# Written VectorE and ScalarE order, deferred elementwise tail, a third output buffer and shorter weight conversion in a fused RWKV6 + tanh-shrink kernel

## Chip, cores, metric

One core of a Trainium2 chip. The metric is the device time of one launch in microseconds (us), the median of the fast runs; an execution counts as slow when it takes over 1.5% longer than the fastest of the same kernel. Ratios are computed as the mean time of one kernel's fast runs over the mean of the other's fast runs of the same rounds, with a 95% interval, so they are not quite the ratio of the medians that are quoted beside them.

## The reference

A linear recurrence with a per-channel decay (RWKV6) feeds a two-layer dense block. All is fp32.

```python
# r, k, v, w: (B=4, H=8, S=768, D=48); u: (H, D); w_in: (384, 2048); w_out: (2048, 384)
for t in range(S):
    cur = einsum('bhd,bhe->bhde', u * k_t, v_t)
    y[:, :, t] = einsum('bhd,bhde->bhe', r_t, state + cur)
    state = w_t[..., None] * state + einsum('bhd,bhe->bhde', k_t, v_t)
x = y as (B*S, H*D)
h = x @ w_in
out = (h - tanh(h)) @ w_out
```

## The kernel before

The 3072 tokens are cut into eight blocks of 384. For each block the kernel runs 16 steps f. A step multiplies the block's x with one 128-column slice of w_in (`hp`), computes g = h - tanh(h) on ScalarE and VectorE, and accumulates g times a slice of w_out (`acc`) two steps later. Beside this, each step does one phase of the *next* block's recurrence: first-level scores, five score levels, transposes, state updates, results. All its matmuls write a PSUM tile named `att`, of which there is one buffer.

A score level: TensorE forms small products of `kq` and `rp`; VectorE copies them under a mask into the score matrix; VectorE then multiplies half of `kq` and half of `rp` by running decay products in place; and only then may TensorE form the next level.

```python
LAG = 2
def level(self, ps, m, p0, n):
    gr = self.gram(ps, self.tiles["kq"], self.tiles["rp"], p0, n, m, L // 2)   # TensorE -> att
    ...
    for h in range(2):
        nc.vector.copy_predicated(out=dst, mask=mask, data=src)               # score copies
def decay(self, m, p0, n):
    for t, half, by in ((self.tiles["kq"], 0, right), (self.tiles["rp"], 1, left)):
        nc.vector.tensor_tensor(out=part, in0=part, op=ALU.mult, in1=by...)    # decay products
    nc.vector.tensor_tensor(out=nxt, in0=left, in1=right, op=ALU.mult)         # next running product

def first(xT, f, ps):
    # three matmuls into hp, then
    nc.scalar.copy(out=h, in_=hp)
    nc.scalar.activation(out=s, in_=h, func=AF.Square)
    # qa, qb, th = tanh(h), big: four more on ScalarE
    nc.vector.scalar_tensor_tensor(out=hs, in0=h, scalar=SERIES, in1=s, ...)   # five operations that make g
    nc.vector.scalar_tensor_tensor(out=hs, in0=qa, ...)
    nc.vector.scalar_tensor_tensor(out=g, in0=qb, ...)
    nc.vector.tensor_tensor(out=th, in0=h, in1=th, op=ALU.subtract)
    nc.vector.copy_predicated(out=g, mask=big, data=th)
    return g
# ... after the last acc of a block:
    o = dense.tile([P, DM], F32, name="o", tag="o")                            # two buffers, three o per block
    nc.scalar.copy(out=o, in_=acc)
    nc.scalar.dma_start(out=out[r0:r0 + P, :], in_=o)

with tc.manual_schedule(engines={PE}):       # TensorE as written, the others by the framework's scheduler
    for i, blk in enumerate(blocks):
        for f in range(NF):
            if ready < NF: load_weights(ready)      # 64-bit weights to fp32: 2 ScalarE, 4 VectorE operations
            g = first(here, f, ps_d)
            next(run, None)                         # one phase of the next block's recurrence
            ...
```

## Time and profile before

| | before |
|---|---|
| median of the fast runs, us | 791.25 (786.39 to 792.87) |
| profiled execution: span, us | 789.3 |
| TensorE, VectorE, ScalarE busy | 88%, 71%, 60% |
| mean granted TensorE clock | 0.949 |
| start and block 0: hp(f=0) of block 1 begins at, us | 168.0 |
| a steady block (mean of blocks 1 to 5), us | 92.3 |

TensorE is busy 88% of the span, but "busy" hides two things: the waits between, and matmuls that run slowly after a wait. So the number to follow is the length of a steady block, from the start of its first hp matmul to the start of the next block's. The prediction below shows the lines. In them PE is TensorE, DVE VectorE, ACT ScalarE, POOL GpSimd and SP SyncE (a q behind the name: a transfer that this engine issues); a line gives start and duration in us, engine, source line, operation, what it writes and reads, shapes and how often, and in brackets the idle time before it and what ended it. The granted clock is the share of TensorE's full clock that the profile shows as allowed.

### The profile page before, as it was taken

How to read it: one execution, taken by the hardware profiler on the slowest of the kernel's cores; microseconds unless marked ns; L12 is line 12 of the kernel's file. 1: busy time of each engine (PE TensorE's matmuls, PEld its weight loads, DVE VectorE, ACT ScalarE, POOL GpSimd, SP SyncE). 2: the span in 40 equal slices, each digit the busy share in tenths (PEclk: the TensorE clock that was granted, in tenths of full speed). 3: DMA queues.
4: the chain of work that ended last, by engine and by line, in shares of the span. 5: the costliest groups of instructions: out<-in, count | busy, mean ns of one | idle time of the engine just before them, and what ended most of it. 6: DMA issues, size and time to landing. Idle time of an engine off the chain costs nothing.

```text
span 789.3 us, 20068 instructions
## 1 busy us (share of the span) xinstructions
PE 695.6 (88%) x8480; PEld 445.4 (56%) x8480; DVE 558.0 (71%) x1138; ACT 470.9 (60%) x955; POOL 18.8 (2%) x49
## 2 busy tenths in 40 slices
PE   3558688897999989997999979999898999999997
PEld 3544455655656556564655556565565656565554
DVE  7988988576775677667775777656777577656664
ACT  3528567375565656566375655655565664757775
POOL 5000000000000000000000000000000000000000
PEclk9988789898999989999899989999899999999999
DMA  8477223123013300133001230133001100000000
GB/s 286 176 238 239 85 81 121 52 71 108 2 41 119 102 12 2 42 119 110 2 10 62 90 112 2 41 115 105 12 2 42 48 32 3 1 9 26 5 0 30
DMA packets 30841, 54.36 MB, mean 69 GB/s; under 512 B 2336, under 2 KB 28704, under 8 KB 30752
## 3 DMA queue, kind: packets, MB, share of 16 engines
q1 hardware_dynamic: 24992, 35.79, 14.2%
q0 software_dynamic: 2304, 12.58, 4.7%
q10 hardware_dynamic: 3456, 4.72, 1.6%
q8 instruction: 66, 1.08, 0.6%
q14 instruction: 23, 0.19, 0.1%
HBM read 47.19 MB, written 4.72 MB: 66 GB/s over the span
## 4 chain that ended last, share of the span: by engine, by line
PE 51%; DVE 14%; ACT 10%; issue 7%; DMA 6%; PEld 5%; PEldq 1%; SPq 0%; ACTq 0%; DVEq 0%
PE acc L450 23%; PE hp L414 20%; PE att L220 6%; DMA out_y<-o 3%; DVE states L300 3%; ACT s L422 2%; DVE gT L436 2%; DVE gT L433 2%; DVE hs L431 2%; ACT h L421 2%; PEld att L315 2%; DMA raw<-in_weights 2%; DVE rp L241 2%; PE att L272 1%; ACT qa L423 1%
## 5 line engine op out<-in xcount | busy, mean ns | idle before, releaser
L450 PE MATMUL acc<-w_sb,gT 128*128 128x384 f32 x768 | 294.1, 521 | 5.4 <-ACT o L454 5.3
L414 PE MATMUL hp<-xT,w_sb 128*128 128x384 f32 x768 | 272.2, 491 | 9.0 <-DVE a L156 6.7
L414 PEld LDWEIGHTS hp<-xT,w_sb 128*128 128x128 f32 x768 | 147.7, 193 | 113.5 <-issue 14.4
L421 ACT COPY h<-hp 128x384 f32<-128x384 f32 x128 | 61.1, 477 | 235.9 <-PE hp L414 235.3
L450 PEld LDWEIGHTS acc<-w_sb,gT 128*128 128x128 f32 x768 | 145.4, 200 | 96.8 <-issue 11.6
L429 DVE SCALAR_TENSOR_TENSOR hs<-h,s 128x384 f32<-128x384 f32 x128 | 71.2, 556 | 163.1 <-ACT s L422 163.0
L220 PE MATMUL att<-rp,kq 48*64 48x32 f32 x3840 | 78.2, 241 | 44.6 <-DVE rp L241 44.0
L220 PEld LDWEIGHTS att<-rp,kq 48*64 48x64 f32 x3840 | 74.2, 161 | 64.7 <-issue 52.8
L436 DVE COPY_PREDICATED gT<-big,th 128x384 f32<-128x384 int32 x128 | 75.4, 589 | 7.7 <-DVE gT L433 0.9
L423 ACT ACTIVATE qa<-s,shift 128x384 f32<-128x384 f32 x128 | 77.0, 601 | 0.3
L433 DVE SCALAR_TENSOR_TENSOR gT<-qb,hs 128x384 f32<-128x384 f32 x128 | 71.3, 557 | 8.2
L424 ACT ACTIVATE qb<-s,shift 128x384 f32<-128x384 f32 x128 | 76.8, 600 | 0.0
L426 ACT ACTIVATE big<-s,shift 128x384 f32<-128x384 f32 x128 | 76.8, 600 | 0.0
L431 DVE SCALAR_TENSOR_TENSOR hs<-qa,hs 128x384 f32<-128x384 f32 x128 | 70.6, 552 | 0.3 <-ACT qa L423 0.3
L435 DVE TENSOR_TENSOR th<-h,th 128x384 f32<-128x384 f32 x128 | 70.5, 551 | 0.0
L422 ACT ACTIVATE s<-h 128x384 f32<-128x384 f32 x128 | 66.9, 523 | 3.6
L425 ACT ACTIVATE th<-h 128x384 f32<-128x384 f32 x128 | 64.9, 507 | 0.0
L263 DVE COPY_PREDICATED scores<-mask,att 128x384 f32<-128x384 uint8 (+1 forms) x72 | 43.5, 617 | 5.7 <-PE att L220 5.5
L241 DVE TENSOR_TENSOR kq<-kq,tot 128x768 f32<-128x768 f32 (+1 forms) x45 | 38.7, 860 | 0.3 <-PE att L220 0.3
L241 DVE TENSOR_TENSOR rp<-rp,tot 128x768 f32<-128x768 f32 (+1 forms) x45 | 38.7, 860 | 0.0
L300 DVE SCALAR_TENSOR_TENSOR states<-states,tot,att 128x48 f32<-128x48 f32 x176 | 34.9, 256 | 2.2 <-PE att L290 2.2
L315 PE MATMUL att<-rp,states 48*64 48x64 f32 x768 | 28.0, 230 | 9.2 <-DVE states L300 9.2
(45 smaller groups left out, 372.6 us busy)
## 6 DMA issues: line engine op xcount, KB each, us to landing
raw<-in_weights POOLq DMA_DIRECT2D x16, 768.0 KB, 4.7
rmix<-in_rT SPq DMA_DIRECT2D x7, 768.0 KB, 4.6
kmix<-in_kT SPq DMA_DIRECT2D x7, 768.0 KB, 6.3
wt<-in_wT SPq DMA_DIRECT2D x7, 768.0 KB, 4.6
kq<-in_kT SPq DMA_DIRECT2D x7, 768.0 KB, 4.5
rp<-in_rT SPq DMA_DIRECT2D x7, 768.0 KB, 4.7
v_sb<-in_v SPq DMA_DIRECT2D x8, 576.0 KB, 6.5
out_y<-o ACTq DMA_DIRECT2D x24, 192.0 KB, 1.9
```

What stands on the lines that cost most here:

```text
L220: nc.tensor.matmul(dst, lhsT=lhs[rows, t0:t0 + L], rhs=src, start=True, stop=True)
L241: nc.vector.tensor_tensor(out=part, in0=part, op=ALU.mult, in1=by.unsqueeze(2).to_broadcast([P, nblk, m]))
L414: nc.tensor.matmul(hp, lhsT=w_in_sb[:, f, kc, :], rhs=xT[:, kc, :], start=(kc == 0), stop=(kc == KC - 1))
L421: nc.scalar.copy(out=h, in_=hp)
L422: nc.scalar.activation(out=s, in_=h, func=AF.Square)
L423: nc.scalar.activation(out=qa, in_=s, func=AF.Square, bias=shift[:, 0:1])
L424: nc.scalar.activation(out=qb, in_=s, func=AF.Square, bias=shift[:, 1:2])
L426: nc.scalar.activation(out=big, in_=s, func=AF.Relu, bias=shift[:, 2:3])
L431: nc.vector.scalar_tensor_tensor(out=hs, in0=qa, scalar=QUAD[0][1], in1=hs, op0=ALU.add, op1=ALU.mult)
L433: nc.vector.scalar_tensor_tensor(out=g, in0=qb, scalar=QUAD[1][1], in1=hs, op0=ALU.add, op1=ALU.mult)
L436: nc.vector.copy_predicated(out=g, mask=big.bitcast(I32), data=th)
L450: nc.tensor.matmul(acc, lhsT=g[:, j * P:(j + 1) * P], rhs=w_out_sb[:, f, :], start=(f == 0), stop=(f == NF - 1))
```

## The change

The intent: keep VectorE from standing in front of TensorE. The five g operations are put off by one step (`rest`), so that they no longer wait for ScalarE in front of the score level; decay products come before score copies; the order is no longer the scheduler's but written, on VectorE and ScalarE; outputs and all other dense tiles have three buffers instead of two; loads for the next block but one are at step 10 (rp at 13); acc lags three steps; the weights are kept times 256, so that a clamp falls away from the conversion. The core of the diff:

```diff
-LAG = 2
+LAG = 3
-    dense = ctx.enter_context(tc.tile_pool(name="dense", bufs=2))
+    dense = ctx.enter_context(tc.tile_pool(name="dense", bufs=3))
...  conversion
-        nc.vector.tensor_scalar(out=a.bitcast(F32), in0=a.bitcast(F32), scalar1=LOWEST,
-                                scalar2=HIGHEST, op0=ALU.max, op1=ALU.min)
         nc.vector.tensor_single_scalar(a, a, 3, op=ALU.logical_shift_left)
...  level
         gr = self.gram(ps, self.tiles["kq"], self.tiles["rp"], p0, n, m, L // 2)
+        self.decay(m, p0, n)
...  first
-        nc.vector.scalar_tensor_tensor(out=hs, in0=h, ...)      # and the four that follow
-        return g
+        def rest():
+            nc.vector.scalar_tensor_tensor(out=hs, in0=h, ...)  # and the four that follow
+        return g, rest
...  main loop
-    with tc.manual_schedule(engines={PE}):
+    with tc.manual_schedule(engines={PE, DVE, ACT}):
-                g = first(here, f, ps_d)
+                g, next_rest = first(here, f, ps_d)
                 waiting.append((second, f, g))
-                next(run, None)
-                if f == PHASES and i + 2 < len(blocks):
-                    blocks[i + 2].load_all()
+                if rest:
+                    rest()
+                rest = next_rest
+                if later:
+                    later.phase(ps_a, f)
+                if after:
+                    after.prepare(f)          # loads at f == 10 and 13, mix and totals at 13
                 if len(waiting) > LAG:
                     s, fs, gs = waiting.pop(0)
                     s.add(fs, gs)
+                if i == 0 and f + AHEAD < NF:
+                    convert(*load_weights(f + AHEAD))
```

Cut from it: masks are built in one tile, zeros of the states are written by VectorE, the six small transfers that complete the first block's x (below, the hole transfers) go out on two queues, the last operations of the conversion change places, and the running decay products of a block are formed ahead of its first step.

More of the change, by code (lines that the diff above doesn't have):

```diff
@@ L42 @@
 PSUM = bass.MemoryType.PSUM
-PE = mybir.EngineType.PE
+PE, DVE, ACT = (getattr(mybir.EngineType, n) for n in ("PE", "DVE", "Activation"))
 B, H, S, D = 4, 8, 768, 48
@@ L61 @@
 BANK = 512
-PHASES = 14
-LAG = 2
+LAG = 3
 SMALL = 0.25
@@ L71 @@
 QUAD = ((0.6848211999739032, 6.0837500747262405), (-2.2310245716004378, 2.349190352486121))
-SCALE = 2.0 ** -48
-LOWEST = float(np.array(896 << 20, np.int32).view(np.float32)) * SCALE
-HIGHEST = float(np.array(1151 << 20, np.int32).view(np.float32)) * SCALE
+UPSCALE = 2.0 ** 8
+HIGH_SCALE = 2.0 ** -111
 @with_exitstack
@@ L96 @@
     xpool = ctx.enter_context(tc.tile_pool(name="xpool", bufs=2))
-    gpool = ctx.enter_context(tc.tile_pool(name="gpool", bufs=LAG + 2))
-    dense = ctx.enter_context(tc.tile_pool(name="dense", bufs=2))
+    gpool = ctx.enter_context(tc.tile_pool(name="gpool", bufs=LAG + 1))
+    dense = ctx.enter_context(tc.tile_pool(name="dense", bufs=3))
     conv = ctx.enter_context(tc.tile_pool(name="conv", bufs=2))
@@ L111 @@
     masks = {}
-    def make_mask(m, width, step):
-        nb = L // (2 * m)
-        t = const.tile([P, nb, width], I8, name=f"mask{m}", tag=f"mask{m}")
-        nc.gpsimd.memset(t, 1.0)
-        for par in range(2):
-            half = t[64 * par:64 * par + 64]
-            nc.gpsimd.affine_select(out=half, in_=half, compare_op=ALU.is_ge, fill=0.0, base=0,
-                                    pattern=[[-2 * m, nb], [0, width]], channel_multiplier=1)
-            nc.gpsimd.affine_select(out=half, in_=half, compare_op=ALU.is_ge, fill=0.0, base=m - 1,
-                                    pattern=[[2 * m, nb], [step, width]], channel_multiplier=-1)
-        masks[m] = t
-    make_mask(1, 2, 1)
+    mask_cols = {1: slice(0, 64), 2: slice(64, 96), 4: slice(96, 128), 8: slice(128, 160),
+                 16: slice(160, 192)}
+    mask_all = const.tile([P, 192], I8, name="mask_all", tag="mask_all")
+    nc.gpsimd.memset(mask_all[0:L], 1.0)
+    for m, at in mask_cols.items():
+        width, step = (2, 1) if m == 1 else (m, 0)
+        nb = L // (2 * m)
+        masks[m] = mask_all[:, at].rearrange("s (b j) -> s b j", j=width)
+        half = masks[m][0:L]
+        nc.gpsimd.affine_select(out=half, in_=half, compare_op=ALU.is_ge, fill=0.0, base=0,
+                                pattern=[[-2 * m, nb], [0, width]], channel_multiplier=1)
+        nc.gpsimd.affine_select(out=half, in_=half, compare_op=ALU.is_ge, fill=0.0, base=m - 1,
+                                pattern=[[2 * m, nb], [step, width]], channel_multiplier=-1)
+        if m == 1:
+            nc.gpsimd.tensor_copy(out=mask_all[L:P, at], in_=mask_all[0:L, at])
+    nc.gpsimd.tensor_copy(out=mask_all[L:P, 64:], in_=mask_all[0:L, 64:])
     A = const.tile([P, 2, NPAIR, NCP, L], F32, name="scores", tag="scores")
     nc.vector.memset(A, 0.0)
-    states = [const.tile([P, NPAIR, NCH, L], F32, name=f"states{q}", tag=f"states{q}")
-              for q in range(NQ)]
+    states = []
+    for q in range(NQ):
+        st = const.tile([P, NPAIR, NCH, L], F32, name=f"states{q}", tag=f"states{q}")
+        nc.vector.memset(st[:, :, :, D:], 0.0)
+        states.append(st)
+    nc.vector.memset(states[0][:, :, 0, :], 0.0)
     w_sb = const.tile([P, NF, 2 * DM], F32, name="w_sb", tag="w_sb")
@@ L150, in load_weights, with convert @@
         up = conv.tile([P, 2 * DM], I32, name="up", tag="up")
-        nc.scalar.activation(out=a.bitcast(F32), in_=hi.bitcast(F32), func=AF.Abs, scale=SCALE)
+        nc.scalar.activation(out=a.bitcast(F32), in_=hi.bitcast(F32), func=AF.Copy, scale=HIGH_SCALE)
         nc.scalar.activation(out=up, in_=lo.bitcast(U32), func=AF.Copy, scale=2.0 ** -29)
-        nc.vector.tensor_scalar(out=a.bitcast(F32), in0=a.bitcast(F32), scalar1=LOWEST,
-                                scalar2=HIGHEST, op0=ALU.max, op1=ALU.min)
+        return f, hi, a, up
+    def convert(f, hi, a, up):
         nc.vector.tensor_single_scalar(a, a, 3, op=ALU.logical_shift_left)
-        nc.vector.tensor_tensor(out=a, in0=a, in1=up, op=ALU.add)
-        nc.vector.scalar_tensor_tensor(out=w_sb[:, f, :].bitcast(I32), in0=hi, scalar=-2 ** 31, in1=a,
+        nc.vector.scalar_tensor_tensor(out=a, in0=hi, scalar=-2 ** 31, in1=a,
                                        op0=ALU.bitwise_and, op1=ALU.bitwise_or)
+        nc.vector.tensor_tensor(out=w_sb[:, f, :].bitcast(I32), in0=a, in1=up, op=ALU.add)
     fence, fences = tc.alloc_semaphore("fence"), []
@@ L230, in level_1, with totals, decay @@
                 data=gr.rearrange("s h (n t) -> s h n t", t=L))
-        def decay(self, m, p0, n):
+        def totals(self, m, p0, n):
+            cols = slice(p0 * NB, (p0 + n) * NB)
+            tot = self.tiles["wt"][:, cols] if m == 1 else self.tots[m, p0]
+            t2 = tot.rearrange("d (n two) -> d n two", two=2)
+            nxt = work.tile([P, n * NB // (2 * m)], F32, name=f"tot{2 * m}_{p0}_{n}", tag=f"tot{2 * m}_{p0}")
+            nc.vector.tensor_tensor(out=nxt, in0=t2[:, :, 0], in1=t2[:, :, 1], op=ALU.mult)
+            self.tots[2 * m, p0] = nxt
+        def decay(self, m, p0, n, which=("kq", "rp")):
             cols = slice(p0 * NB, (p0 + n) * NB)
@@ L237, in decay @@
             t2 = tot.rearrange("d (n two) -> d n two", two=2)
-            left, right = t2[:, :, 0], t2[:, :, 1]
-            for t, half, by in ((self.tiles["kq"], 0, right), (self.tiles["rp"], 1, left)):
-                part = t[:, cols].rearrange("d (n two m) -> d n two m", two=2, m=m)[:, :, half, :]
-                nc.vector.tensor_tensor(out=part, in0=part, op=ALU.mult,
-                                        in1=by.unsqueeze(2).to_broadcast([P, nblk, m]))
-            nxt = work.tile([P, nblk], F32, name=f"tot{2 * m}_{p0}_{n}", tag=f"tot{2 * m}_{p0}")
-            nc.vector.tensor_tensor(out=nxt, in0=left, in1=right, op=ALU.mult)
-            self.tots[2 * m, p0] = nxt
+            for name in which:
+                half = 0 if name == "kq" else 1
+                part = self.tiles[name][:, cols].rearrange(
+                    "d (n two m) -> d n two m", two=2, m=m)[:, :, half, :]
+                by = t2[:, :, 1 - half].unsqueeze(2).to_broadcast([P, nblk, m])
+                nc.vector.tensor_tensor(out=part, in0=part, in1=by, op=ALU.mult)
         def level(self, ps, m, p0, n):
             gr = self.gram(ps, self.tiles["kq"], self.tiles["rp"], p0, n, m, L // 2)
+            self.decay(m, p0, n)
             nb = L // (2 * m)
@@ L340, in result, with fill_holes @@
                 nc.scalar.copy(out=dst.rearrange("e (c a t) -> e c a t", a=2, t=L), in_=src)
-        def fill_holes(self):
+        def fill_holes(self, engines):
             for n in range(2 * KC):
@@ L346, in fill_holes @@
                 src = 64 * (n // KC) + 16 * (n % KC)
-                nc.sync.dma_start(out=self.xT[64 * h + D:64 * h + 64, i, :],
-                                  in_=self.late[src:src + 16, :])
-        def load_all(self):
-            for name, src in (("rmix", rT), ("kmix", kT), ("wt", wT), ("kq", kT), ("rp", rT)):
-                self.load(name, src, 0, NPAIR)
-            self.load_v()
-        def phases(self, ps):
-            self.mix(0, NPAIR, False)
-            for p0 in (0, UP):
-                self.level_1(ps, p0)
-                yield
-            m = 1
-            while m < L:
-                self.decay(m, 0, NPAIR)
-                m *= 2
-                if m < L:
-                    self.level(ps, m, 0, NPAIR)
-                    yield
-            for p0 in (0, UP):
-                self.turn(ps, p0)
-                yield
-                self.update(ps, p0, True)
-                yield
-            for p0 in (0, UP):
-                self.result(ps, p0)
-                yield
-            self.fill_holes()
-            yield
+                engines[n % len(engines)].dma_start(out=self.xT[64 * h + D:64 * h + 64, i, :],
+                                                    in_=self.late[src:src + 16, :])
@@ new lines, in phase @@
+        def phase(self, ps, k):
+            if k < 2:
+                self.level_1(ps, k * UP)
+                if k == 1:
+                    self.decay(1, 0, NPAIR, ("rp",))
+            elif k < 7:
+                self.level(ps, 2 ** (k - 1), 0, NPAIR)
+            elif k < 11:
+                p0 = (k - 7) // 2 * UP
+                if k % 2 == 1:
+                    self.turn(ps, p0)
+                else:
+                    self.update(ps, p0, True)
+            elif k < 13:
+                self.result(ps, (k - 11) * UP)
+                if k == 12:
+                    self.fill_holes([nc.sync])
@@ new lines, in prepare @@
+        def prepare(self, k):
+            if k == 10:
+                for name, src in (("rmix", rT), ("kmix", kT), ("wt", wT), ("kq", kT)):
+                    self.load(name, src, 0, NPAIR)
+                self.load_v()
+            elif k == 13:
+                self.load("rp", rT, 0, NPAIR)
+                self.mix(0, NPAIR, False)
+                for m in (1, 2, 4, 8, 16, 32):
+                    self.totals(m, 0, NPAIR)
+            elif k == 14:
+                self.decay(1, 0, NPAIR, ("kq",))
@@ L389, in start @@
                 self.level_1(ps, p0)
-            for m in (2, 4, 8, 16):
-                make_mask(m, m, 0)
+                self.decay(1, p0, UP)
+                self.totals(1, p0, UP)
             yield
-            m = 1
-            while m < L:
+            for m in (2, 4, 8, 16, 32):
                 for p0 in (0, UP):
-                    self.decay(m, p0, UP)
-                    if 2 * m < L:
-                        self.level(ps, 2 * m, p0, UP)
-                m *= 2
+                    self.level(ps, m, p0, UP)
+                    self.totals(m, p0, UP)
                 yield
@@ L406, in start @@
                 self.result(ps, p0)
-            self.fill_holes()
+            self.fill_holes([nc.sync, nc.scalar])
             yield
@@ L420, in first @@
         h, th, s, qa, qb, big = (new(n) for n in ("h", "th", "s", "qa", "qb", "big"))
-        nc.scalar.copy(out=h, in_=hp)
+        nc.scalar.activation(out=h, in_=hp, func=AF.Copy, scale=1.0 / UPSCALE)
         nc.scalar.activation(out=s, in_=h, func=AF.Square)
@@ L428, in first @@
         g = gpool.tile([P, NB], F32, name="gT", tag="gT")
-        nc.vector.scalar_tensor_tensor(out=hs, in0=h, scalar=SERIES, in1=s,
-                                       op0=ALU.mult, op1=ALU.mult)
-        nc.vector.scalar_tensor_tensor(out=hs, in0=qa, scalar=QUAD[0][1], in1=hs,
-                                       op0=ALU.add, op1=ALU.mult)
-        nc.vector.scalar_tensor_tensor(out=g, in0=qb, scalar=QUAD[1][1], in1=hs,
-                                       op0=ALU.add, op1=ALU.mult)
-        nc.vector.tensor_tensor(out=th, in0=h, in1=th, op=ALU.subtract)
-        nc.vector.copy_predicated(out=g, mask=big.bitcast(I32), data=th)
-        return g
+        def rest():
+            nc.vector.scalar_tensor_tensor(out=hs, in0=h, scalar=SERIES, in1=s,
+                                           op0=ALU.mult, op1=ALU.mult)
+            nc.vector.scalar_tensor_tensor(out=hs, in0=qa, scalar=QUAD[0][1], in1=hs,
+                                           op0=ALU.add, op1=ALU.mult)
+            nc.vector.scalar_tensor_tensor(out=g, in0=qb, scalar=QUAD[1][1], in1=hs,
+                                           op0=ALU.add, op1=ALU.mult)
+            nc.vector.tensor_tensor(out=th, in0=h, in1=th, op=ALU.subtract)
+            nc.vector.copy_predicated(out=g, mask=big.bitcast(I32), data=th)
+        return g, rest
     class Second:
@@ L453, in add @@
                     o = dense.tile([P, DM], F32, name="o", tag="o")
-                    nc.scalar.copy(out=o, in_=acc)
+                    nc.scalar.activation(out=o, in_=acc, func=AF.Copy, scale=1.0 / UPSCALE)
                     r0 = self.row0 + j * P
                     nc.scalar.dma_start(out=out[r0:r0 + P, :], in_=o)
-    with tc.manual_schedule(engines={PE}):
-        blocks = [Block(b, q) for b in range(B) for q in range(NQ)]
-        ready = 0
-        with tc.tile_pool(name="ps_boot", bufs=4, space=PSUM) as boot:
-            xT = blocks[0].begin()
-            for i, _ in enumerate(blocks[0].start(boot)):
-                if i == 0:
-                    for st in states:
-                        nc.gpsimd.memset(st, 0.0)
-                if i % 2 == 1:
-                    load_weights(ready)
-                    ready += 1
-            blocks[1].load_all()
-        ps_d = ctx.enter_context(tc.tile_pool(name="ps_d", bufs=1, space=PSUM))
-        ps_a = ctx.enter_context(tc.tile_pool(name="ps_a", bufs=1, space=PSUM))
-        waiting = []
-        for i, blk in enumerate(blocks):
-            here, run = xT, iter(())
-            if i + 1 < len(blocks):
-                xT = blocks[i + 1].begin()
-                run = blocks[i + 1].phases(ps_a)
@@ new lines @@
+    blocks = [Block(b, q) for b in range(B) for q in range(NQ)]
+    AHEAD = 4
+    with tc.manual_schedule(engines={PE}), \
+            tc.tile_pool(name="ps_boot", bufs=4, space=PSUM) as boot:
+        xT = blocks[0].begin()
+        for i, _ in enumerate(blocks[0].start(boot)):
+            if i % 2 == 1:
+                convert(*load_weights(i // 2))
+        blocks[1].prepare(10)
+    ps_d = ctx.enter_context(tc.tile_pool(name="ps_d", bufs=1, space=PSUM))
+    ps_a = ctx.enter_context(tc.tile_pool(name="ps_a", bufs=1, space=PSUM))
@@ L479 @@
+    with tc.manual_schedule(engines={PE, DVE, ACT}):
+        for k in (13, 14):
+            blocks[1].prepare(k)
+        waiting, rest, half_done = [], None, []
+        for i, blk in enumerate(blocks):
+            here = xT
+            later = blocks[i + 1] if i + 1 < len(blocks) else None
+            after = blocks[i + 2] if i + 2 < len(blocks) else None
+            if later:
+                xT = later.begin()
             second = Second(blk.b * S + blk.q * NB, ps_d)
             for f in range(NF):
-                if ready < NF:
-                    load_weights(ready)
-                    ready += 1
@@ L484 @@
-                g = first(here, f, ps_d)
+                g, next_rest = first(here, f, ps_d)
                 waiting.append((second, f, g))
-                next(run, None)
-                if f == PHASES and i + 2 < len(blocks):
-                    blocks[i + 2].load_all()
+                if rest:
+                    rest()
+                rest = next_rest
+                if later:
+                    later.phase(ps_a, f)
+                if after:
+                    after.prepare(f)
@@ L491 @@
                     s.add(fs, gs)
-            assert next(run, None) is None
+                if i == 0 and f + AHEAD < NF:
+                    convert(*load_weights(f + AHEAD))
+        rest()
         for s, fs, gs in waiting:
```

## The prediction

> **What bounds the kernel now.** I read the chain that ended last first (TensorE 51% of it, two matmul lines alone 43%), then the busy time of each engine by stretch, then who waited for whom, then the timeline of one steady block. A block is 384 tokens, 16 steps f. Each step has three first-layer matmuls (hp), some work of the next block's recurrence (att) and three second-layer matmuls (acc).
>
> Busy time by stretch: us, then busy us of PE, PEld, DVE, ACT and POOL, then the granted TensorE clock, DMA share and GB/s:
>
> ```profile
> 57.00:178.00 121.00, 102.58 (x1161) 64.95 (x1162) 98.08 (x190) 76.09 (x145) 4.78 (x9) 0.85 0.35 112
> 363.00:456.00 93.00, 84.97 (x1069) 53.85 (x1068) 63.63 (x133) 55.20 (x116) 0.00 (x0) 0.96 0.18 58
> 727.00:789.30 62.30, 56.24 (x173) 32.33 (x171) 37.10 (x70) 42.87 (x88) 0.00 (x0) 0.98 0.05 19
> ```
>
> The first row is mostly block 0, which also converts weights: VectorE is 81% busy and the clock is low. The second is a steady block: TensorE busy, VectorE at 68%. The third is mostly the last block, which has no recurrence beside it. From the TensorE timeline, hp(f=0) of blocks 0 to 7 starts at 57.0, 168.0, 260.7, 352.5, 445.3, 537.1, 629.7 and 716.8. So blocks 1 to 5 take 91.7 to 92.9 us each, block 6, beside which nothing is loaded for a later one, 87, and 72.5 us remain from the start of block 7 to the end.
>
> One steady block, TensorE only (start, us, what, number, idle before it and its releaser):
>
> ```profile
> 368.32 0.91 PE L450 MATMUL acc<-w_sb,gT 128*128 128x384 f32 x2 [1.05 <-ACT o L454]
> ...
> 374.72 2.79 PE L220 MATMUL att<-rp,kq 48*64 48x32 f32 x96 [3.55 <-DVE rp L241]
> 377.43 4.00 PE L450 MATMUL acc<-w_sb,gT 128*128 128x384 f32 x6
> 381.27 2.10 PE L414 MATMUL hp<-xT,w_sb 128*128 128x384 f32 x6
> 383.30 1.60 PE L220 MATMUL att<-rp,kq 48*64 48x32 f32 x96
> 384.83 2.20 PE L450 MATMUL acc<-w_sb,gT 128*128 128x384 f32 x6
> 386.87 2.10 PE L414 MATMUL hp<-xT,w_sb 128*128 128x384 f32 x6
> 389.72 1.60 PE L220 MATMUL att<-rp,kq 48*64 48x32 f32 x96 [0.75 <-DVE rp L241]
> ...
> 411.34 0.85 PE L272 MATMUL att<-ident,kq 128*128 128x128 f32 x6 [0.91 <-DVE states L300]
> ...
> 422.55 1.61 PE L315 MATMUL att<-rp,states 48*64 48x64 f32 x48 [1.58 <-DVE states L300]
> ```
>
> The bracketed idle times sum to 7.84 us. After the 3.55 us one, the same work is slower: att 2.79 instead of 1.60 (+1.19), acc 4.00 instead of 2.20 (+1.80). Together 10.8 us of a 92.5 us block. The origin is on ScalarE:
>
> ```profile
> 364.29 0.48 ACT L421 COPY h<-hp 128x384 f32<-128x384 f32 x1 [1.23 <-PE hp L414]
> 367.79 0.48 ACT L454 COPY o<-acc 128x384 f32<-128x384 f32 x1 [3.02 <-DMA out_y<-o]
> 368.17 0.53 ACT L422 ACTIVATE s<-h 128x384 f32<-128x384 f32 x1
> 368.72 0.56 DVE L429 SCALAR_TENSOR_TENSOR hs<-h,s 128x384 f32<-128x384 f32 x1 [4.54 <-ACT s L422]
> 373.62 0.95 DVE L241 TENSOR_TENSOR rp<-rp,tot 128x768 f32<-128x768 f32 x1
> ```
>
> The third output copy of a block finds both o buffers still being written out. ScalarE is in order, so s(f) behind it is late. VectorE is in order, its next item needs that s, and score copies and decay products stand behind it. So the decay ends at 374.6 and att starts at 374.72. Over the run:
>
> ```profile
> PE att L220 <- DVE rp L241: 44.0, 18, 7.4
> ...
> ACT o L454 <- DMA out_y<-o: 15.1, 6, 3.0
> ...
> PE att L315 <- DVE states L300: 9.2, 7, 2.3
> ...
> PE att L272 <- DVE states L300: 6.7, 7, 2.3
> ```
>
> **What the Trainium skill says.** "TensorE: Matmul & The Clock Gate", Part 1, says that an idle window of about 3.4 us puts the array at half clock until some 3.4 us of sustained work. The trace agrees: 2.79 against 1.60 us after 3.55 us idle, no slowing after 0.75. "DMA: Bandwidth & Descriptors" names a fixed cost of about 2 us, mostly the write receipt: the last output lands 1.9 us after issue, but those at block ends, beside two 768 KB loads, after 4.7 to 5.1. "Perfetto Trace Analysis", Engine Utilization, says that the same gap repeating can mean too few buffers; the o wait comes once per block, 6 times. "VectorE: DVE Perf Modes", The DRAIN you can't avoid, holds that a semaphore between chained operations costs nothing. The trace differs: independent 384-wide operations start 0.47 us apart, but the predicated copy starts 0.66 after the gT that it depends on, in the tail as well (780.91, 781.57).
>
> **The change, part by part.** The order listing confirms that TensorE keeps its instructions; only acc moves one step later (lag 3), and the same sequence is written for VectorE and ScalarE.
>
> (a) Three o buffers: the 3.0 us ScalarE wait and the 1.05 us TensorE wait go. The loads also move to steps 10 to 13, away from the output at step 2.
>
> (b) In a level step VectorE now does the five g operations of the step before, two decay products, two score copies. Start to start: products 0.86 each = 1.72; copies 0.47 each = 0.94 (1.62 for m=2, whose copies start 0.81 apart in this trace); the five g operations now have three dependent neighbours, 2 x 0.47 + 3 x 0.66 = 2.92. Sum 5.6. TensorE's level step is also 5.6 (383.30 to the would-be 388.9), so VectorE keeps up without slack in total. The link that matters is short: from the end of att, decay and copies need 1.72 + 0.94 + about 0.1 = 2.8 us (3.5 for m=2), while the next att comes 2.04 + 2.03 = 4.07 us later. The g operations come after, with ScalarE's chain done. I expect the decay wait to vanish.
>
> (c) State updates (12 x 0.175 = 2.1 us) no longer stand between g operations waiting for ScalarE: 2.1 + 0.1 fits into the 4.07 us before the transpose or result needs them. The 0.91 and 1.58 vanish.
>
> (d) So a steady block becomes its TensorE steps, start to start as the timeline has them where nothing waits: 5 level steps at 5.60 = 28.0; 2 first-level at 4.93 = 9.9; 2 transposes at 4.62 = 9.2; 2 updates at 4.92 = 9.8; 2 results at 6.58 = 13.2; 3 dense at 3.87 = 11.6. Sum 81.7. I take 82.2 for small waits. Blocks 1 to 6 took 548.8; six at 82.2 are 493: 56 us gained.
>
> (e) Weights. The min/max goes: 16 x about 0.5 = 8 us of VectorE, half of it before or in block 0's path. One conversion left is shift 0.66, sign 1.05, add 0.87 = 2.6. Block 0's level steps become 5.6 + 2.6 = 8.2 us against TensorE's 5.6: VectorE bounds there. Stepping it by hand from hp(0): steps 0 to 6 end (last decay) at about 53; conversions, g and two state updates carry result(11) to about 79; two results and three dense steps end near 102. Before it took 111. Gain 9. ScalarE (3.0 for a chain, 1.7 for a conversion) stays below.
>
> (f) Start: one min/max less in each of four conversions and one add later (2.8 us). The xT copies no longer stand behind a conversion that waits 2.77 us for raw. Six hole transfers go on two queues instead of one. hp(0), begun at 57.0 and whole only after 61, I put at 53.
>
> (g) End: lag 3 leaves four acc groups after the last hp instead of three, +1.9; the o waits of this stretch (1.02 at step 2, 1.03 at the end) go. Fifteen steps of 3.87, five groups of 1.94 and 3.9 from the last matmul to the end: 71.6 against 72.5.
>
> Sum: 53 + 102 + 493 + 71.6 = 719.6. The estimates of block 0 and the start add dependent costs generously, so I put **718 us**, 9% less.
>
> **Rivals.** R1: VectorE becomes the bound in steady blocks too. Its level step is 5.6 against 5.6; if copies or dependent pairs cost 0.5 us more, five steps in seven blocks add some 17 us: 735. For: the fixed order cannot fill an idle moment with something else. Against: steps outside the levels have 1 to 2 us to spare, and only the short link is on TensorE's path. R2: the fixed ScalarE order makes a new wait. Score and ks copies of steps 6 to 10 now stand behind the whole activation chain (3.0 us), ending at 3.8 to 4.6 us after hp against needs at 4.7 to 5.6; in block 0 the conversion waits there for raw. If 1 us per such step is lost, five per block: about 750. Against: before, ks was copied behind the chain as well (403.90, needed at 405.45) without a wait. R3: the TensorE waits were caused by the o wait alone, and orders matter little: then three buffers give the same block, and the total is about the same 720; only experiments tell these apart. R4: loads from step 10 on (3.6 MB, about 4.6 us per 768 KB, so some 22 us) hold back the hole transfers, wanted within 12 us of step 12; if hp(0) waits 3 us per block: 736.
>
> **Range and chances.** The floor is 53 + 95 + 490 + 70 = 708, with a few us for a faster start: 702. R1 or R4 at full size gives 735 to 738. Range **703 to 738**. Slower would need every saved wait to return; within 2% means above 774, beyond even R2: faster 0.96, same 0.03, slower 0.01.
>
> **What would show it.** Right: blocks of 82 us; no o wait on the output; att waiting for rp under 10 us in all; 2.79 us att gone from steady blocks; clock near 0.99; first hp near 53; block 0 near 102 with VectorE over 85% busy. Wrong: steady blocks over 86 us, with att waiting for scores or rp (R1), for ScalarE's scores or ks (R2), or hp for the hole transfers (R4).

## The result

| | before | after |
|---|---|---|
| median of the fast runs, us | 791.25 | 725.56 (722.68 to 728.44) |
| ratio | 1 | 0.918 (0.912 to 0.924) |
| profiled span, us | 789.3 | 722.9 |
| mean granted TensorE clock | 0.949 | 0.982 |
| first hp begins at, us | 57.0 | 56.95 |
| block 0, us | 111.0 | 103.9 |
| a steady block (mean of blocks 1 to 5), us | 92.3 | 81.6 |
| start of block 6 to the end, us | 159.8 | 154.2 |

Of the 66.4 us between the two profiled spans, blocks 1 to 5 give 5 x 10.7 = 53.7, the start and block 0 give 7.1, the rest 5.6.

Busy time by stretch in the kernel after (columns as in the prediction): block 0, the first steady block, the last block.

```profile
57.00:161.00 104.00, 86.69 (x1035) 54.82 (x1036) 90.45 (x159) 72.73 (x132) 5.30 (x10) 0.89 0.36 122
161.00:242.50 81.50, 81.29 (x1070) 51.80 (x1069) 66.13 (x133) 57.05 (x116) 0.00 (x0) 1.00 0.20 66
650.00:722.90 72.90, 68.59 (x212) 39.55 (x210) 45.96 (x85) 53.17 (x106) 0.00 (x0) 0.99 0.05 17
```

In the steady block TensorE is busy for all but 0.2 us, at full clock. In block 0 VectorE is busy 90.45 of 104 us, more than TensorE's 86.69; a_minmax below, which lengthens VectorE's work alone, confirms that it bounds there.

The steady block's level steps on TensorE, kernel after:

```profile
178.36 1.60 PE L226 MATMUL att<-rp,kq 48*64 48x32 f32 x96
179.89 2.20 PE L468 MATMUL acc<-w_sb,gT 128*128 128x384 f32 x6
181.93 2.10 PE L429 MATMUL hp<-xT,w_sb 128*128 128x384 f32 x6
183.96 1.60 PE L226 MATMUL att<-rp,kq 48*64 48x32 f32 x96
```

No bracket is left: no idle time in front of any of them, no att of 2.79 us, no acc of 4.00. Steps are 5.60 us apart. VectorE in the same stretch:

```profile
180.80 0.95 DVE L258 TENSOR_TENSOR kq<-kq,tot 128x768 f32<-128x768 f32 x1
181.66 0.95 DVE L258 TENSOR_TENSOR rp<-rp,tot 128x768 f32<-128x768 f32 x1
182.53 1.02 DVE L277 COPY_PREDICATED scores<-mask_all,att 128x384 f32<-128x384 uint8 x2
183.46 0.55 DVE L446 SCALAR_TENSOR_TENSOR hs<-h,s 128x384 f32<-128x384 f32 x1
184.12 0.56 DVE L448 SCALAR_TENSOR_TENSOR hs<-qa,hs 128x384 f32<-128x384 f32 x1
184.78 0.56 DVE L450 SCALAR_TENSOR_TENSOR gT<-qb,hs 128x384 f32<-128x384 f32 x1
185.25 0.55 DVE L452 TENSOR_TENSOR th<-h,th 128x384 f32<-128x384 f32 x1
185.91 0.59 DVE L453 COPY_PREDICATED gT<-big,th 128x384 f32<-128x384 int32 x1
186.40 0.94 DVE L258 TENSOR_TENSOR kq<-kq,tot 128x768 f32<-128x768 f32 x1
```

From one kq product to the next it is 186.40 - 180.80 = 5.60 us, without a wait: VectorE has no slack in a level step either. But what TensorE needs (decay and copies) is done first, at about 183.5, and the next att at 183.96 finds it ready, with 0.4 us to spare. The g operations come behind it and are wanted only three steps later.

### The profile page after: what moved, and what is told of

It is laid out like the page before. It is cut to its first block, busy times and chain, and to the rows that moved or that the text cites. A ratio compares the mean times of both kernels' runs of the same rounds, so it can differ in the third digit from the quotient of the medians.

```text
span 722.9 us, 20014 instructions
## 1 busy us (share of the span) xinstructions
PE 674.0 (93%) x8480; PEld 433.6 (60%) x8480; DVE 570.6 (79%) x1125; ACT 486.1 (67%) x955; POOL 12.5 (2%) x35
## 4 chain that ended last, share of the span: by engine, by line
PE 62%; PEld 11%; DVE 9%; issue 7%; ACT 2%; PEldq 2%; DMA 1%; ACTq 0%; DVEq 0%
PE acc L468 27%; PE hp L429 25%; PE att L226 7%; PEld hp L429 4%; PEld acc L468 3%; PEld att L329 2%; PEldq L335 2%; DVE states L314 1%; DVE w_sb L164 1%; DVE a L162 1%; PE att L345 1%; PEld att L345 1%; PE att L304 1%; PEld att L304 1%; DMA raw<-in_weights 1%
## 5 line engine op out<-in xcount | busy, mean ns | idle before, releaser
L468 PE MATMUL acc<-w_sb,gT 128*128 128x384 f32 x768 | 279.6, 501 | 0.0
L468 PEld LDWEIGHTS acc<-w_sb,gT 128*128 128x128 f32 x768 | 140.1, 192 | 84.7 <-issue 2.4
L436 ACT ACTIVATE h<-hp 128x384 f32<-128x384 f32 x128 | 62.4, 487 | 174.3 <-PE hp L429 171.6
L226 PEld LDWEIGHTS att<-rp,kq 48*64 48x64 f32 x3840 | 68.0, 147 | 41.0 <-issue 33.3
L226 PE MATMUL att<-rp,kq 48*64 48x32 f32 x3840 | 72.9, 231 | 20.1 <-DVE rp L258 7.6
L438 ACT ACTIVATE qa<-s,shift 128x384 f32<-128x384 f32 x128 | 78.8, 616 | 4.2
L314 DVE SCALAR_TENSOR_TENSOR states<-states,tot,att 128x48 f32<-128x48 f32 x176 | 32.2, 256 | 13.9 <-PE att L304 13.9
L277 DVE COPY_PREDICATED scores<-mask_all,att 128x384 f32<-128x384 uint8 (+1 forms) x72 | 40.2, 619 | 0.0
L329 PEld LDWEIGHTS att<-rp,states 48*64 48x64 f32 x768 | 25.8, 144 | 10.4 <-issue 10.4
```

Of the source, the lines that this page charges most:

```text
L226: nc.tensor.matmul(dst, lhsT=lhs[rows, t0:t0 + L], rhs=src, start=True, stop=True)
L438: nc.scalar.activation(out=qa, in_=s, func=AF.Square, bias=shift[:, 0:1])
L468: nc.tensor.matmul(acc, lhsT=g[:, j * P:(j + 1) * P], rhs=w_out_sb[:, f, :], start=(f == 0), stop=(f == NF - 1))
```

## The experiments

Every kernel was correct. The runs were made on several chips, in rounds in which the kernel before took 789.8 to 793.6 us, so small differences between rows are read from the trace columns. "1st block" is the time at which hp(f=0) of block 1 begins, so start and block 0 together; "steady" is the mean of blocks 1 to 5.

| run | us | ratio to before | 1st block | steady |
|---|---|---|---|---|
| kernel before | 791.3 | 1 | 168.0 | 92.3 |
| kernel after | 725.6 | 0.918 | 160.9 | 81.6 |
| b_three_out | 767.6 | 0.970 | 168.3 | 88.1 |
| b_defer_three | 743.4 | 0.941 | 160.7 | 86.1 |
| a_no_defer | 788.2 | 0.994 | 162.0 | 93.0 |
| a_free_no_defer | 760.7 | 0.959 | (profile slow) | |
| a_free_order | 715.1 | 0.903 | 147.9 | 82.3 |
| a_two_out | 725.5 | 0.916 | 161.0 | 81.6 |
| a_copies_first | 727.5 | 0.918 | (profile slow) | |
| a_minmax | 733.4 | 0.930 | 169.4 | 81.6 |
| a_ahead6 | 723.8 | 0.917 | 160.3 | 81.5 |
| a_holes | 721.2 | 0.911 | 156.4 | 81.6 |
| a_mixed | **710.3** | **0.897** | 146.0 | 81.6 |
| a_mixed_holes | 712.9 | 0.903 | 148.5 | 81.6 |

Names that begin with b are the kernel before with something added; those with a are the kernel after with something undone or moved.

### Was it the output wait alone? b_three_out and a_two_out

```diff
 b_three_out (before)      a_two_out (after): the same line with bufs=2
-                    o = dense.tile([P, DM], F32, name="o", tag="o")
+                    o = dense.tile([P, DM], F32, name="o", tag="o", bufs=3)
```

> The kernel before with a third output buffer and nothing else. My theory (order and buffers share the gain): the 3.0 us ScalarE wait and the 1.05 us TensorE wait at each block's step 2 go; the decay wait behind it shrinks from 3.55 to about 1.4 us, because copies and g operations still stand before the decay, and the clock no longer drops; 0.75, 0.91 and 1.58 stay. About 6 of the 10.8 us of a block, seven times: about 750 us, blocks of 86. Rival R3 (the output wait alone was the cause): blocks of 82 and about 735 or less.

767.6 us: the third buffer alone gives 24 us of the 66, less than I expected (750), and far less than R3 needed. In a steady block the output waits are gone, the others stay:

```profile
362.90 1.63 PE L220 MATMUL att<-rp,kq 48*64 48x32 f32 x96 [2.07 <-DVE rp L241]
364.46 3.83 PE L450 MATMUL acc<-w_sb,gT 128*128 128x384 f32 x6
...
398.19 0.84 PE L272 MATMUL att<-ident,kq 128*128 128x128 f32 x6 [0.91 <-DVE states L300]
...
409.27 1.61 PE L315 MATMUL att<-rp,states 48*64 48x64 f32 x48 [1.46 <-DVE states L300]
```

The decay wait shrank from 3.55 only to 2.07 us, and acc is still slow after it (3.83 instead of 2.20). A wait shorter than the 3.4 us that I had taken as the threshold was enough here to lose 1.6 us of clock. It need not be: the wait of 2.00 us at 187.85 in the same trace is followed by an acc of 2.20.

> The changed kernel with two output buffers again. My theory: outputs now leave at step 2, far from the loads, and land in about 2.4 us, so the third copy would wait some 1.2 us on ScalarE, which has slack, and VectorE has the deferred g of the step before to do: no TensorE wait, 723 to 731 us. R3: the gain of the third buffer is lost again, 30 us or more: over 755.

725.5 us, as my theory had it. In the new program two buffers would do. ScalarE still waits for a buffer, about 2 us instead of the 1.2 expected, and in the steady blocks nothing feels it (81.6 us):

```profile
179.75 0.49 ACT L472 ACTIVATE o<-acc 128x384 f32<-128x384 f32 x1 [2.29 <-DMA out_y<-o]
```

Only behind the last block, where nothing follows, does it cost anything: the third copy waits 1.02 us for the buffer, and start of block 6 to the end is 155.5 us instead of 154.2. So the third buffer is worth 24 us in the old program and no measurable time in the new one. Gains of parts do not add: the rest of the change takes away what this wait had cost. Which part of it does so, the deferral most likely, was not run apart.

### Was it the deferral? a_no_defer, a_free_no_defer, b_defer_three

```diff
 a_no_defer; a_free_no_defer is this with manual_schedule(engines={PE}) as well
-                if rest:
-                    rest()
-                rest = next_rest
+                next_rest()
```

> The changed kernel, its order still written, but the five g operations of a step are written in that step ahead of the decay instead of one step later. My theory: VectorE then stands until ScalarE's chain ends (3.1 us after hp), so decay and copies end about 6.6 us after hp against 5.6 wanted, about 1 us of TensorE wait in each of seven steps of seven blocks, and more in block 0: about 775 us. If a written order as such was the gain: 726 within 1%.

788.2 us, nearly all of the gain gone, and steady blocks of 93.0. The mechanism is the expected one, its size bigger than my 775. One level step, VectorE and TensorE:

```profile
363.54 0.56 DVE L446 SCALAR_TENSOR_TENSOR hs<-h,s 128x384 f32<-128x384 f32 x1 [1.45 <-ACT s L437]
...
366.03 0.58 DVE L453 COPY_PREDICATED gT<-big,th 128x384 f32<-128x384 int32 x1
366.51 0.95 DVE L258 TENSOR_TENSOR kq<-kq,tot 128x768 f32<-128x768 f32 x1
...
370.24 1.67 PE L226 MATMUL att<-rp,kq 48*64 48x32 f32 x96 [2.22 <-DVE scores L277]
371.84 3.86 PE L468 MATMUL acc<-w_sb,gT 128*128 128x384 f32 x6
```

g stands in front of the decay, is paced by ScalarE from 363.54 to 366.5, and the next att waits 2.22 us. A written order as such is therefore no gain: with g in the wrong place it is as slow as before.

> Scheduler's order on VectorE and ScalarE, and the g operations in program order in their own step (not deferred); third buffers, load places, lag 3, decay ahead of copies kept. Theory A: the deferral is what places g behind the decay for the scheduler too; without it blocks of 85 to 88 and about 745 us. Theory B: the scheduler reorders anyhow, so that the deferral matters only to a written order: 715 within 1%, like the scheduler's order with deferral.

760.7 us from three fast runs: Theory A (its 745 was too low). With the scheduler's order too, putting g one step later in the program is worth 760.7 - 715.1 = 46 us; with the written order, 788.2 - 725.6 = 63 us. The profiled execution of this kernel (1729.9 us) is not used.

> The kernel before with two things only: the third output buffer (767.6 us alone) and the five g operations moved one step later in program order, orders left to the scheduler. Theory A (the deferral is the main part of the change): decay waits go, blocks of 82.5 to 84, but start and block 0 as before: about 735 us. Theory B (load places, decay ahead of copies or lag 3 are needed too): 755 to 767.

743.4 us, between the two theories. Two of the parts, buffer and deferral, in an otherwise old kernel make 48 of the 66 us; the deferral alone, with two buffers, was not run. A steady block keeps 86.1 us, with two decay waits:

```profile
351.53 2.49 PE L220 MATMUL att<-rp,kq 48*64 48x32 f32 x96 [2.01 <-DVE rp L241]
...
366.81 1.60 PE L220 MATMUL att<-rp,kq 48*64 48x32 f32 x96 [0.75 <-DVE rp L241]
```

In front of the first of them, ScalarE does a `rmix` product of a later block ahead of s, and VectorE, after 2.13 us of waiting for that s, takes two g operations, both copies and a third g operation ahead of the first decay product, and a fourth between the two products (345.98 to 351.38). Whether the load places, the decay written ahead of the copies, or the lag removes these two waits in the new program, no run tells apart. The other dense tiles, which have two buffers here and three in the new program, are an unlikely cause: from block 1 to block 5 the trace lists no wait of ScalarE for VectorE.

### What is the written order worth? a_free_order and a_mixed

```diff
 a_free_order
-    with tc.manual_schedule(engines={PE, DVE, ACT}):
+    with tc.manual_schedule(engines={PE}):
 a_mixed
+        with tc.manual_schedule(engines={PE} if i == 0 else {PE, DVE, ACT}):
```

> The changed kernel with VectorE and ScalarE left to the scheduler's order again, all else kept (deferred g, three buffers, lag 3, loads at step 10). My theory: a part of the decay and state waits returns, blocks of 84 to 87: about 745 us. If order matters little: 726 within 1%.

715.1 us: my theory falls. The order that gives the change its name makes it 10 us slower. Steady blocks are 0.8 us longer without it (82.3), so it does gain there, about 5 us in six blocks; but block 1 begins at 147.9 instead of 160.9. The reason can be read in block 0. VectorE in the kernel after, one level step with the conversion of a later weight slice in its written place:

```profile
94.07 0.95 DVE L258 TENSOR_TENSOR kq<-kq,tot 128x768 f32<-128x768 f32 x1
94.93 0.95 DVE L258 TENSOR_TENSOR rp<-rp,tot 128x768 f32<-128x768 f32 x1
95.80 1.02 DVE L277 COPY_PREDICATED scores<-mask_all,att 128x384 f32<-128x384 uint8 x2
96.73 0.55 DVE L161 TENSOR_SCALAR a<-a 128x768 int32<-128x768 int32 x1
97.31 0.96 DVE L162 SCALAR_TENSOR_TENSOR a<-raw,a 128x768 int32<-128x768 int32 x1
98.41 0.96 DVE L164 CUSTOM_DVE_ANT_0 w_sb<-a,up 128x1536 uint16<-128x1536 uint16 x1
...
102.01 0.94 DVE L258 TENSOR_TENSOR kq<-kq,tot 128x768 f32<-128x768 f32 x1
```

7.94 us per step, the conversion taking 99.28 - 96.73 = 2.55 of them (the g operations left out begin at 99.28). The weights that it makes are wanted four steps later, the decay at once. The scheduler moves such pieces: in its order the last three level steps follow at TensorE's own pace (86.61, 92.21 and 97.81 us, 5.60 apart). Its trace differs in three ways: two slices more are converted around the first hp (done at 53.1 and 60.6), three conversions instead of five end within the level steps, and single conversion operations stand between dependent g operations, so that neighbours start 0.47 us apart instead of 0.58. a_ahead6 below tests the first; the other two were not run apart.

> Scheduler's order in block 0, written order from block 1 on. If the written order gains 0.8 us in each of six steady blocks and loses 16 us in block 0 (103.9 against 88.1), this gets both: first hp near 58, block 0 of 88, blocks of 81.6: about 709 us. If the gain of the free order lay elsewhere (its tail, its start): 715 or more.

710.3 us, as expected: the scheduler's order where VectorE bounds, the written one where TensorE does. This version beats both kernels. Block 0 takes 88.0 us, the steady blocks 81.6. Its TensorE in block 0:

```profile
84.06 1.60 PE L226 MATMUL att<-rp,kq 48*64 48x32 f32 x96
85.59 2.20 PE L468 MATMUL acc<-w_sb,gT 128*128 128x384 f32 x6
87.63 2.10 PE L429 MATMUL hp<-xT,w_sb 128*128 128x384 f32 x6
89.66 1.60 PE L226 MATMUL att<-rp,kq 48*64 48x32 f32 x96
```

### Decay ahead of copies? a_copies_first

```diff
         gr = self.gram(...)
-        self.decay(m, p0, n)
         ...                                    # score copies
+        self.decay(m, p0, n)
```

> The changed kernel with the score copies ahead of the decay products in each level step. My theory: the next att needs both the decay and the free PSUM bank, and their sum stays 2.8 us against 4.07, so the order of the two does not matter: 723 to 730 us, blocks of 81.6. If decay ahead of copies is what gains: blocks longer by 0.9 us in each of five steps, some 30 us in all, about 755.

727.5 us from three fast runs, ratio 0.918 like the kernel after. In the written order it makes no difference which of the two comes first, as expected. The reason given, that the next att waits for both, is not shown by a trace: the profiled execution was slow, 3812.6 us, and is not used.

### The conversion: a_minmax and a_ahead6

```diff
 a_minmax
     def convert(f, hi, a, up):
+        nc.vector.tensor_scalar(out=a, in0=a, scalar1=-1.0e30, scalar2=1.0e30, op0=ALU.max, op1=ALU.min)
 a_ahead6
-    AHEAD = 4
+    AHEAD = 6
+        for f in (4, 5):                       # ahead of the first step
+            convert(*load_weights(f))
```

> The changed kernel with one more VectorE operation of 768 columns per conversion (a clamp that clamps nothing), as the kernel before has. In the written order 9 to 10 of the 12 conversions of block 0 lie on VectorE's path: 0.5 to 0.66 us each, and about 1 us in the start: block 0 of 109 to 110, total 731 to 732 us. If conversions are hidden: 725 within 2.

733.4 us: one VectorE operation more per conversion costs 8 us, a little more than expected, all of it before block 1. A level step of block 0 is 8.53 us instead of 7.94. So the removed clamp was worth about that much in the written order.

> The changed kernel, written order, with two conversions more ahead of the first step, where VectorE stood idle for 11.8 us waiting for the holes. If that idle time is a part of what the scheduler's order uses in block 0: two conversions of 2.6 us fewer on VectorE's path, block 0 of 99 instead of 104, about 720 us. If block 0 is long for another reason: 725 within 2.

723.8 us, about 2 us less instead of 5, within what runs of one kernel differ by. I had mis-stepped it. Starting two conversions earlier removes those of steps 10 and 11, but the level steps keep theirs (att at 89.92, 97.87 and 105.81 us, still 7.9 apart); only the wait of the first result shrank, from 2.74 to 1.35 us. So the two slices converted early are the small part of what the scheduler gains; the rest must lie in where it puts the others, and no run shows which of the two ways counts.

### The start: a_holes and a_mixed_holes

```diff
 a_holes: SP written too in the start, loads for block 1 placed by hand
-        blocks[1].prepare(10)                  # rmix, kmix, wt, kq, v; then rp
+            ...                                # rmix, kmix after i == 1, wt after 5, kq after 7
+        blocks[1].load_v()                     # v and rp behind the six hole transfers
+        blocks[1].load("rp", rT, 0, NPAIR)
```

> The changed kernel with the loads of rp and v for block 1 issued behind the six hole transfers of the start instead of ahead of them. If those two loads (1.3 MB) are what makes the 24 KB transfers land 5 us after issue: landing near 2.5 us, first hp near 54 instead of 57, total 722 to 724. If it is a fixed cost of such small transfers: no change, 726.

721.2 us, 4.4 less than the kernel after, as expected or a little better. In the kernel after, the two loads go out just ahead of the six transfers of 24 KB, and hp waits:

```profile
49.89 0.37 SPq L181 DMA_DIRECT2D rp<-in_rT  x1
...
50.98 0.37 SPq L188 DMA_DIRECT2D v_sb<-in_v  x1
...
51.88 1.86 SPq L361 DMA_DIRECT2D xT<-late  x3
51.88 2.14 ACTq L361 DMA_DIRECT2D xT<-late  x3
```

The first hp begins at 56.95, 5.1 us after the transfers begin to be issued. With the loads behind, issue at 51.51 and first hp at 53.89: 2.4 us. (In a_two_out and a_no_defer, whose start is that of the kernel after, it is 5.1 to 5.2 us again.) Block 1 begins 4.5 us sooner: VectorE carries 3.0 us of it through block 0, and the rest comes at step 11, where TensorE's two groups of result matmuls are slow in the kernel after (2.42 and 1.53 us) and not here (1.61 and 0.89).

> Scheduler's order in block 0, written order after it, and the two loads behind the hole transfers. If the two gains add (15 and 4.4 us): first hp near 54, block 0 of 88, 706 us. If VectorE is what block 0 waits for, an earlier first hp is taken back there: block 0 of 91 to 92 and 710 us.

712.9 us: the two gains do not add, for another reason than the one I gave. The first hp did not come earlier (57.99 us; 58.06 in a_mixed). In the scheduler's order a weight load takes the place of the two that were moved, and the transfers are late again:

```profile
51.54 0.53 POOL L152 DMA_DIRECT2D raw<-in_weights  x1 [10.85 <-DVE tot L244]
...
52.06 1.85 SPq L361 DMA_DIRECT2D xT<-late  x3
52.06 2.13 ACTq L361 DMA_DIRECT2D xT<-late  x3
...
57.99 1.62 PE L430 MATMUL hp<-xT,w_sb 128*128 128x384 f32 x2 [6.88 <-DMA xT<-late]
```

Block 0 is 2.5 us longer besides (90.5 against 88.0): the scheduler places its VectorE operations differently, and two level steps wait 3.91 and 1.00 us for score copies, where those of a_mixed wait 3.04 and 0.21.

## Why the prediction was right, point by point

- **Total, 718 against 725.6.** Inside the range, and faster as said. By its own sum in the profiled run: start 53 (measured 56.95), block 0 102 (103.9), six blocks 493 (489.3), end 71.6 (72.7). That the sum is so near is in part luck: three terms are 7 us too short together, and the fourth is 3.7 too long.
- **(d) the steady block, 82.2.** Measured 81.6: the bare sum of TensorE's steps, 81.7, was right, and there were next to no small waits; (c)'s two waits are gone too. The waits listed one by one in the prediction are the whole difference between the two blocks.
- **(b) the level step.** Right to the digit: 5.6 us on both engines. The short link (decay and copies) holds, but more narrowly than predicted: from the end of att at 179.96 to that of the copies at 183.55 it takes 3.6 us and not 2.8 of the 4.07, since VectorE has the g operations in hand until 180.80. The dependent spacing of 0.66 us was used rightly in the steady block; in block 0 most such pairs are 0.58 to 0.6 us apart.
- **(a) and R3, the third buffer.** I gave it a part of its own. a_two_out shows that it has none in the new program's steady blocks: what it repairs, the rest of the change has made harmless. Alone in the old program it is worth 24 us. R3 is refuted both ways.
- **(e) block 0.** The bound (VectorE) and the size were right. That the written order itself caused it was not seen: the prediction took that order as given, and 16 us of block 0 were to be had (a_free_order, a_mixed). Half of 8 us was too little for the clamp on the path: a_minmax shows 8.
- **(f) the start: the term that was mis-sized.** 53 us predicted, 56.95 measured. Two reasons. The six transfers land late because of loads issued just before them (a_holes: 3 us). And the states that end earlier on VectorE (46.4 us instead of 48.5) bring nothing: the recurrence's last result matmuls end at 50.9 us against 50.3 before, since the first result's matmuls stand in between on TensorE and are slow (the group begun at 46.84 takes 1.53 us, against 0.89 before).
- **(g) the end.** The 0.9 us gain did not come: 72.7 us against 72.5 before.
- **Readings that were off.** Blocks 1 to 5 before take 91.6 to 93.0 us, and one output at a block end landed after 5.7 us. "No slowing after 0.75" holds, but the same trace has an att after 1.75 us of waiting, at 648.84, that is followed by an acc of 3.86 us; the clock rule that the prediction took over was too simple.
- **R1** did not come, though VectorE has no slack: its order puts the needed work first. **R2** and **R4** did not come: no hp waits for a hole transfer after block 0, and no att of a steady block waits for ScalarE.

What the prediction did not single out is the main part. It spoke of the deferral only as what lets g "come after"; the runs show that it is worth 46 us in the scheduler's order and 63 in the written one, and that the written order by itself costs 10. What stays open: which of the load places (with the work moved beside them), the decay written first and the lag takes a scheduled block from 86.1 us (b_defer_three) to 82.3 (a_free_order).

## What to carry to other kernels

On an in-order engine, ask of each operation who waits for it and how soon: put what the bounding engine needs first, and put off by one iteration what waits for a third engine. Writing an order by hand pays where one engine bounds and its needs are known; where another engine is saturated, as in a first block with extra work, the hand-written place of that extra work can cost more than the rest gains. Parts that repair the same wait do not add, so undo each in the new program before calling it a gain.

## What the Trainium skill lacked or had wrong

- "VectorE: DVE Perf Modes", The DRAIN you can't avoid: from eight copies it concludes that a semaphore between chained operations costs nothing extra. Here 384-wide operations start 0.47 us apart when independent (184.78 to 185.25) and 0.58 to 0.66 when one reads what the one before wrote (183.46 to 184.12). The five g operations of a level step take 2.94 us (183.46 to 186.40); at 0.47 each they would take 2.35, an estimate, so an independent operation between two dependent ones is worth having.
- "TensorE: Matmul & The Clock Gate", Part 1: the loss can begin sooner than with a gap of about 3.4 us. Gaps of 2.07 (b_three_out) and 2.22 us (a_no_defer) were followed by an acc group of 3.83 and 3.86 us instead of 2.20; of two gaps of 2.28 us in block 0 of the kernel after, that at 96.97 was followed by 2.20 and that at 104.92 by 3.88. So a short gap is a risk, not a rule. The same part does say that frequent short idles between groups of matmuls make the clock swing, but not how long or how frequent.
- No page that I found gives a figure for a small transfer behind large ones: the 24 KB transfers of the start let the first hp begin 5.1 us after issue behind 1.3 MB of loads (kernel after), 2.4 us without them (a_holes).
- Two executions, of two kernels on one chip (a_free_no_defer, a_copies_first), took 1729.9 and 3812.6 us; three others of each were fast. In the second a mean acc matmul took 2390 ns, against 501 in the kernel after, while a kq product of VectorE took 868 against 861 ns; the cause is not known. I found no page with such a state of a whole execution.
